# A scan and mixture-of-experts kernel: 64x64 quarters, 1/q0 by ScalarE, three routed groups

## The chip, the cores and the metric

The kernel runs on one core of a Trainium2 chip. A core has TensorE (PE: matmuls, with the weight load shown apart as PEld), VectorE (DVE), ScalarE (ACT), GpSimd (POOL) and SyncE (SP, which here only issues DMAs). Each engine works through its own instructions in the order in which they are written; between engines there are semaphores. Matmuls write to PSUM, which has eight banks of 512 fp32 values per partition; VectorE and ScalarE read it. The metric is device time in microseconds: three runs of the kernel before gave 320.64, 321.75 and 328.07 us, median 321.75.

## The reference, cut to what matters

```python
B, H, S, D = 4, 8, 768, 48                    # r, k, v, w: [B, H, S, D]; u: [H, D]
state = zeros(B, H, D, D)
for t in range(S):
    cur = einsum('bhd,bhe->bhde', u * k_t, v_t)
    y[:, :, t] = einsum('bhd,bhde->bhe', r_t, state + cur)
    state = w_t[..., None] * state + einsum('bhd,bhe->bhde', k_t, v_t)
x = y as rows: [B * S = 3072, H * D = 384]
skip = x @ w_skip > 0                         # only these rows are computed further
e = argmax(x @ w_gate); gate = softmax(x @ w_gate)[e]     # 8 experts
out = x + skip * gate * (relu(x @ w1[e]) @ w2[e])         # w1: 384 x 1024, w2: 1024 x 384
```

All tensors are fp32.

## The kernel before, in words

The recurrence is done in chunks of 128 positions: 4 batches of 6 chunks, 24 in all, all 8 heads at once. Within a chunk, `q` is the product of the decays w from a position to the chunk's end (a scan backwards, L277), `rh` the product from the chunk's start (a scan forwards, L289), `rq` = 1/q0 with q0 the whole chunk's product (L284). Then `kq` = k * q (L287, GpSimd), `rp` = r * rq * rh (L297, VectorE, one operation for each of the four head pairs), and the scores of a chunk are kq^T rp, masked to the positions before (L334). Tiles hold head pair a (0 to 3) in the free dimension and the two heads g of a pair in partitions 0 to 63 and 64 to 127, 48 rows of each in use.

A chunk's y comes together in one PSUM bank `psy`: VectorE first writes the bonus term there (L347: the sums over d of u r k, made by TensorE in bank `psb` from the block-diagonal ones-times-u tile `ubk_sb`, L343, times v transposed, `vt`), TensorE adds scores times v (L378, two heads side by side in the column halves of the array) and state times rp (L383, block-diagonal state `sblk`, the full array). ScalarE copies it out (`evict`, L388), TensorE turns it into rows and multiplies by the gate weights at once (`rows_out`, L396, two partial logits added later), and ScalarE and SP store the rows (`store`). The state lives in PSUM bank `psu` (L356 adds to it, L366 scales it by the next chunk's q0, L371 copies it into `sblk`).

The eight PSUM banks in this stage are psu, psY, psA0, psA1 (scores of heads g = 0 and 1), psB, pss (routing) and two of tag psT (transposes and rows).

The order on all engines is written out by hand (`manual_schedule`, L592 to L660): step s holds the state update and outputs of chunk s, the scores, masks and bonus of chunk s + 1, the scans of chunk s + 2, the loads of chunk s + 4, and the store of chunk s - 1. In step s VectorE's order is: scan q, reciprocal, scan rh, rp (for s + 2), two masks and the bonus (for s + 1). ScalarE's is: store copies (s - 1), state scalings and copies (s), the y copy (s), the transposed keys (s + 1), the check of w (s + 2). TensorE's is: state update, y (s), key transposes, scores and bonus sums (s + 1), rows (s). `later` holds routers, small chains of VectorE operations over a group of chunks that `drip(k)` emits between the others, k at a time; `flush` emits what they want of the other engines. `GROUPS` says after which chunks a router starts: after 6, 12, 18 and 24. For the first two groups the one-hot tiles of token positions are made by ScalarE (`mark`, two activations each, two chunks a step), for the others by VectorE (`one_hot`, L476). `beside` makes a GpSimd operation wait for a VectorE operation, so that the two don't begin at a bad time for each other: `rk` = r * k (L302) for the last rp, the weight split of L273 for the last routing operation.

After the 24 chunks the last group is routed beside the first expert's matmuls, and then the experts follow (L739 on): gathers of rows, matmuls in three passes of split weights, scatters. Their weights are loaded and split partly during the chunks (L652 to L660). That part uses the banks again, by their tags (L753).

## Time and profile before

| what | us |
|---|---|
| runs, median (lowest to highest) | 321.75 (320.64 to 328.07) |
| the profiled execution, whole | 317.5 |
| its span, first to last instruction | 315.6 |
| busy: TensorE, VectorE, ScalarE, GpSimd | 292.2, 244.8, 185.3, 115.5 |

The profile is of one execution. Lines such as L297 are lines of the kernel before. A busy time is the sum over instructions, of which successive ones can overlap; the mean of one is its whole duration. The chain of waits is followed back from the last instruction: at each step to what released it, or to the instruction before it on its engine; its rows are start, length, engine, tile written, line and number of instructions. In the rows of groups, the part after the second bar is the engine's idle time just before these instructions, and what ended it. fp32 matmuls are issued as two instructions each, so four matmuls show as x8. The granted clock of TensorE was 0.986 on average.

### The profile page before, as it was taken

The page shows a single profiled execution, that of the slowest core. Times are in us where ns is not written, and L with a number is a line of the kernel's source. Part 1 is how long each engine was busy: PE and PEld are TensorE (multiplying, and loading weights), DVE is VectorE, ACT ScalarE, POOL GpSimd, SP SyncE. Part 2 cuts the span into 40 slices and gives each one's busy share as a digit, 9 for nine tenths or more (in the row PEclk, how much of TensorE's full clock was granted, in tenths as well). Part 3 has the DMA queues.
Part 4 walks back from the last instruction along what each step waited for, and adds up shares of the span by engine and source line. Part 5 has one row for each costly group of instructions (what it writes and reads, how often), then busy time and mean ns, then how long its engine had stood idle before and what let it go on. Part 6 is the DMA issues. An engine that isn't in the chain of part 4 may idle for free.

```text
span 315.6 us, 8456 instructions
## 1 busy us (share of the span) xinstructions
PE 292.2 (93%) x3229; PEld 269.6 (85%) x3229; DVE 244.8 (78%) x505; ACT 185.3 (59%) x527; POOL 115.5 (37%) x118
## 2 busy tenths in 40 slices
PE   7499999899898998979999999999999999999992
PEld 2388888788787887868889899999999999999991
DVE  8899999999999999999637479587785949496310
ACT  4437667689775998766633358274564828184200
POOL 8164455555535566543401772411102020101111
PEclk9879999999999999999999999999999999999998
DMA  7999999999899988885301489756657473630001
GB/s 227 220 214 241 232 292 271 257 264 264 212 233 257 267 187 179 180 206 194 116 25 34 143 294 348 275 195 218 213 199 239 152 256 95 243 143 27 6 4 37
DMA packets 23778, 60.45 MB, mean 192 GB/s; under 512 B 4902, under 2 KB 11338, under 8 KB 23728
## 3 DMA queue, kind: packets, MB, share of 16 engines
q1 hardware_dynamic: 21248, 53.69, 62.6%
q0 software_dynamic: 2048, 5.48, 5.3%
q8 instruction: 27, 0.44, 0.7%
q10 hardware_dynamic: 432, 0.66, 0.6%
q14 instruction: 23, 0.19, 0.2%
HBM read 52.76 MB, written 7.86 MB: 192 GB/s over the span
## 4 chain that ended last, share of the span: by engine, by line
PE 72%; DMA 13%; DVE 10%; POOL 1%; issue 1%; ACT 1%; SPq 0%; POOLq 0%; DVEq 0%
DMA wrk<-wrk 10%; PE psO L790 7%; PE psO L788 7%; PE psO L789 7%; PE psY L378 6%; PE psH L770 6%; PE psH L769 6%; PE psH L768 6%; PE psA L328 6%; PE psY L383 5%; PE psB L343 5%; DVE asb L334 4%; PE psH L126 4%; DVE psY L347 3%; PE psT L321 3%; DVE rp L297 2%
## 5 line engine op out<-in xcount | busy, mean ns | idle before, releaser
L775 ACT ACTIVATE hh<-psH 128x256 fp32r<-128x256 f32 x60 | 23.0, 383 | 56.8 <-PE psH L770 53.5
L732 POOL DMA_INDIRECT out<-fin,ids x16 | 17.0, 1065 | 102.5 <-DVE fin L795 94.7
L770 PE MATMUL psH<-xTh,w1l 128*128 128x256 f32 x168 | 47.6, 283 | 0.0
L769 PE MATMUL psH<-xTl,w1h 128*128 128x256 f32 x168 | 47.6, 283 | 0.0
L768 PE MATMUL psH<-xTh,w1h 128*128 128x256 f32 x168 | 47.6, 283 | 0.0
L302 POOL TENSOR_TENSOR rk<-wrk 128x512 f32<-128x512 f32 x24 | 30.6, 1275 | 28.9 <-DVE rp L297 14.5
L788 PE MATMUL psO<-w2h,hh 128*128 128x384 f32 x120 | 40.8, 340 | 0.0
L790 PE MATMUL psO<-w2h,hl 128*128 128x384 f32 x120 | 40.2, 335 | 0.0
L789 PE MATMUL psO<-w2l,hh 128*128 128x384 f32 x120 | 40.2, 335 | 0.0
L378 PE MATMUL psY<-asb,v 128*48 128x128 f32 x384 | 26.6, 282 | 13.1 <-DVE psY L347 13.0
L287 POOL TENSOR_TENSOR kq<-wrk,q 128x512 f32<-128x512 f32 x24 | 28.6, 1190 | 18.5 <-DVE q L277 13.4
L776 DVE SCALAR_TENSOR_TENSOR hl<-psH,hh 128x256 fp32r<-128x256 f32 x60 | 25.2, 420 | 12.5 <-ACT hh L775 12.1
L334 DVE TENSOR_TENSOR asb<-psA,c_sb 128x512 f32<-128x512 f32 x48 | 30.7, 681 | 4.3 <-PE psA L328 4.3
L378 PEld LDWEIGHTS psY<-asb,v 128*48 128x48 f32 x384 | 20.5, 126 | 15.6 <-DVE psY L347 15.4
L297 DVE SCALAR_TENSOR_TENSOR rp<-wrk,rq,rh 128x128 f32<-128x128 f32 x96 | 33.1, 405 | 0.5
L770 PEld LDWEIGHTS psH<-xTh,w1l 128*128 128x128 f32 x168 | 32.2, 192 | 0.0
L769 PEld LDWEIGHTS psH<-xTl,w1h 128*128 128x128 f32 x168 | 32.2, 192 | 0.0
L768 PEld LDWEIGHTS psH<-xTh,w1h 128*128 128x128 f32 x168 | 32.2, 192 | 0.0
L795 DVE SCALAR_TENSOR_TENSOR fin<-psO,gates,xg 128x384 f32<-128x384 f32 x15 | 9.3, 618 | 28.5 <-PE psO L790 28.5
L289 DVE TENSOR_TENSOR_SCAN rh<-wrk,pss 128x516 f32<-128x516 f32 x24 | 28.9, 1205 | 2.6 <-PE pss L516 1.3
L277 DVE TENSOR_TENSOR_SCAN q<-wrk,pss 128x516 f32<-128x516 f32 x24 | 29.1, 1214 | 1.4 <-DMA wrk<-wrk 1.4
L343 PE MATMUL psB<-rk,ubk_sb 128*128 128x128 f32 x192 | 27.8, 288 | 0.9 <-POOL rk L302 0.9
(145 smaller groups left out, 668.6 us busy)
## 6 DMA issues: line engine op xcount, KB each, us to landing
r<-w SPq DMA_DIRECT2D x48, 512.0 KB, 5.8
wrk<-wrk SPq DMA_DIRECT2D x46, 288.9 KB, 6.3
v<-vN SPq DMA_DIRECT2D x24, 192.0 KB, 6.2
out<-x SPq DMA_DIRECT2D x24, 192.0 KB, 5.4
vt<-wrk SPq DMA_DIRECT2D x46, 96.0 KB, 6.1
wrk<-wrk SPq DMA_DIRECT2D x1, 258.5 KB, 3.8
wrk<-wrk ACTq DMA_DIRECT2D x1, 256.0 KB, 4.0
wrk<-wrk SPq DMA_DIRECT2D x1, 256.0 KB, 4.5
```

The lines of the kernel that those rows point to most:

```text
L277: nc.vector.tensor_tensor_scan(q.rearrange("p a j -> p (a j)")[:, ::-1], t[:, 1:1 + NP * CW][:, ::-1], floor, 0.0, op0=ALU.mult, op1=ALU.max)
L297: last = nc.vector.scalar_tensor_tensor(rp[:, a], wk["r"][:, a], wk["rq"][:, a], wk["rh"][:, a, :P], op0=ALU.mult, op1=ALU.mult)
L302: mul = nc.gpsimd.tensor_tensor(rk.rearrange("p a j -> p (a j)"), wk["w"][:, R_OFF:K_OFF], wk["w"][:, K_OFF:V_OFF], op=ALU.mult)
L334: nc.vector.tensor_tensor(s, psa[g], tri.rearrange("p (o j) -> p o j", o=1).to_broadcast([P, NP, P]), op=ALU.mult)
L343: nc.tensor.matmul(wk["psb"][:, a], ubk_sb[:, a], wk["rk"][:, a], start=True, stop=True)
L378: nc.tensor.matmul(psy[64 * g:64 * g + D, a], v[:, 2 * a + g], wk["asb"][g][:, a], start=False, stop=(c == 0), skip_group_check=True)
L768: nc.tensor.matmul(ps, w1h[:, o:o + P], xTh[:, kc], start=(kc == 0), stop=False)
L769: nc.tensor.matmul(ps, w1h[:, o:o + P], xTl[:, kc], start=False, stop=False)
L770: nc.tensor.matmul(ps, w1l[:, o:o + P], xTh[:, kc], start=False, stop=(kc == KC - 1))
L788: nc.tensor.matmul(pso, h[j, fc][0], w2h[:, o], start=(fc == 0), stop=False)
L789: nc.tensor.matmul(pso, h[j, fc][0], w2l[:, o], start=False, stop=False)
L790: nc.tensor.matmul(pso, h[j, fc][1], w2h[:, o], start=False, stop=(fc == FC - 1))
```

## The change

- **Quarters.** `ubk_sb` and `sblk` lose their zero blocks (64 columns, not 128). The bonus sums (L343) and state times rp (L383) become eight matmuls each on 64x64 quarters of the array, where they were four on the full array.
- **y in two banks.** `psy` becomes a bank for each g (tags psY0, psY1), with head pair a = 2 * c2 + a2 at partition half c2 and column block a2. To pair with this, `vt` is laid out so too (four loads per chunk where there were two, each in pieces of 1 KB where there were 2 KB, issued one step later), `wgp_sb` as well (twelve loads at the start where there were three), and `store` puts the columns back. The bonus and the y copy become two operations each, one for each bank. The score matmuls of L378 are ordered by bank.
- **The bonus sums' place.** The bank psB goes: the sums are written into columns 64 to 127 of each head pair in psA0 and psA1, after the masks have read these. `bonus_sums` and `bonus` move from step s - 1 to step s, after the state update, and the bonus stands ahead of the scan q on VectorE.
- **1/q0 by ScalarE.** `scale_reads` makes r * rq by four ScalarE activations, after `evict` in ScalarE's order; VectorE then makes rp by one tensor_tensor with rh in place.
- **Order.** `rows_out` moves from the end of step s to the start of step s + 1. `intra` is split: `turn` (key transposes and their copy) comes ahead of the outputs, `scores` where `intra` was.
- **State copy.** One ScalarE copy of 128x192 in place of two of 64x192.
- **Routers.** Groups of 9, 9 and 6 chunks. All one-hots by VectorE; `mark` goes. `drip`'s pace at the late group is 3, before 2. The split of L273 waits for the bonus of its step, in place of the last routing operation.

```diff
-GROUPS = ((0, 6), (6, 6), (12, 6), (18, 6))
+GROUPS = ((0, 9), (9, 9), (18, 6))
+GM = 9
...
+        def load_vt(i):
+            b, c = seq[i]
+            vt = vt_sb[i % (NBUF + 1)]
+            for c2 in range(2):
+                for g in range(2):
+                    o = V_OFF + 2 * c2 * P
+                    nc.sync.dma_start(vt[64 * c2:64 * c2 + D, 2 * g:2 * g + 2],
+                                      wrk[b, c, g, :, o:o + 2 * P])
...
-        psy = ps1.tile([P, NP, P], F32, tag="psY", name="psY")
+        psy = [ps1.tile([P, 512], F32, tag=f"psY{g}", name=f"psY{g}") for g in range(2)]
+        psy3 = [z[:, :2 * P].rearrange("p (b j) -> p b j", b=2) for z in psy]
...
-                mul = nc.gpsimd.tensor_tensor(lo, raw, hi, op=ALU.subtract)
-                if vec.last is not None:
-                    beside(mul, vec.last)
+                beside(nc.gpsimd.tensor_tensor(lo, raw, hi, op=ALU.subtract), work[i - 2]["bonus"])
...
-        def prep_reads(i):
+        def scale_reads(i):
             wk = work[i]
             rp = wk["rp"] = att.tile([P, NP, P], F32, tag="rp", name=f"rp{i}", bufs=3)
             for a in range(NP):
-                last = nc.vector.scalar_tensor_tensor(
-                    rp[:, a], wk["r"][:, a], wk["rq"][:, a], wk["rh"][:, a, :P],
-                    op0=ALU.mult, op1=ALU.mult)
+                nc.scalar.activation(rp[:, a], wk["r"][:, a], AF.Copy, scale=wk["rq"][:, a])
+
+        def prep_reads(i):
+            wk = work[i]
+            rp = wk["rp"]
+            last = nc.vector.tensor_tensor(rp, rp, wk["rh"][:, :, :P], op=ALU.mult)
...
+        psb = [z.rearrange("p a (h j) -> p a h j", h=2)[:, :, 1] for z in psa]
+
         def bonus_sums(i):
-            wk = work[i]
-            wk["psb"] = ps1.tile([P, NP, P], F32, tag="psB", name=f"psB{i}")
-            for a in range(NP):
-                nc.tensor.matmul(wk["psb"][:, a], ubk_sb[:, a], wk["rk"][:, a],
-                                 start=True, stop=True)
+            rk = work[i]["rk"].rearrange("p a (h j) -> p a h j", h=2)
+            for a2 in range(2):
+                for c2 in range(2):
+                    for g in range(2):
+                        a, rows = 2 * c2 + a2, slice(64 * g, 64 * g + HP)
+                        nc.tensor.matmul(psb[g][64 * c2:64 * c2 + HP, 2 * a2:2 * a2 + 2],
+                                         ubk_sb[rows, a], rk[rows, a], start=True, stop=True)
 
         def bonus(i):
-            nc.vector.tensor_tensor(psy, work[i]["psb"], vt_sb[i % (NBUF + 1)], op=ALU.mult)
+            vt = vt_sb[i % (NBUF + 1)].rearrange("p a (h j) -> p (a h) j", h=2)
+            for g in range(2):
+                work[i]["bonus"] = nc.vector.tensor_tensor(
+                    psy[g][:, :2 * P].rearrange("p (q j) -> p q j", j=HP), psb[g],
+                    vt[:, 4 * g:4 * g + 4], op=ALU.mult)
...
             if c > 0:
-                for a in range(NP):
-                    nc.tensor.matmul(psy[:, a], sblk[i % 2][:, a], wk["rp"][:, a],
-                                     start=False, stop=True, skip_group_check=True)
+                for a2 in range(2):
+                    for c2 in range(2):
+                        for g in range(2):
+                            a, rows = 2 * c2 + a2, slice(64 * g, 64 * g + HP)
+                            nc.tensor.matmul(psy3[g][64 * c2:64 * c2 + D, a2],
+                                             sblk[i % 2][rows, a, :D], wk["rp"][rows, a],
+                                             start=False, stop=True, skip_group_check=True)
 
         def evict(i):
-            xT = work[i]["xT"] = att.tile([P, NP, P], F32, tag="xT", name=f"xT{i}")
-            nc.scalar.copy(xT, psy)
+            xT = work[i]["xT"] = att.tile([P, 2 * 2, P], F32, tag="xT", name=f"xT{i}")
+            for g in range(2):
+                nc.scalar.copy(xT[:, 2 * g:2 * g + 2], psy3[g])
...
                 if on(s - 1):
+                    rows_out(s - 1)
                     store(s - 1)
+                if on(s):
+                    update(s)
+                    carry(s)
+                    bonus_sums(s)
+                drip(pace[0])
                 for i0, m in GROUPS:
                     if i0 + m == s:
-                        pace[0] = 1 if i0 + m < LATE else 2
+                        pace[0] = 1 if i0 + m < LATE else 3
                         later.append(router(i0, m))
                         if i0 + m == LATE:
                             later.append(early())
                 if on(s):
-                    update(s)
-                    carry(s)
-                drip(pace[0])
+                    bonus(s)
                 if on(s + 2):
                     prep_scan(s + 2)
+                if on(s + 1):
+                    turn(s + 1)
+                flush()
                 if on(s):
                     outputs(s)
-                flush()
                 if on(s + 2):
                     prep_keys(s + 2)
                     drip(2 * pace[0])
-                    prep_reads(s + 2)
                 if on(s):
                     evict(s)
+                if on(s + 2):
+                    scale_reads(s + 2)
+                    prep_reads(s + 2)
                 if on(s + 1):
-                    intra(s + 1)
+                    scores(s + 1)
                     mask(s + 1, 0)
                     mask(s + 1, 1)
-                    bonus_sums(s + 1)
-                    bonus(s + 1)
                     drip(2 * pace[0])
                 if on(s + 2):
                     prep_check(s + 2)
-                for _ in range(min(2, len(marks))):
-                    marks.popleft()()
                 if s == n - 1:
                     early_tokens(0)
-                if on(s):
-                    rows_out(s)
                 flush()
```

162 lines of the change are left out of this document (75 added, 87 removed).

## The prediction

> **What bounds the kernel now.** I read the engine totals first, then a table of stretches, then the chain of waits, then the groups by shape and a timeline of two steps.
>
> ```profile
> span 315.6 us, 8456 instructions
> PE 292.2 (93%) x3229; PEld 269.6 (85%) x3229; DVE 244.8 (78%) x505; ACT 185.3 (59%) x527; POOL 115.5 (37%) x118
> ...
> 15.00:60.00 45.00, 43.00 (x642) 37.91 (x643) 42.73 (x83) 28.99 (x96) 24.18 (x21) 0.94 1.05 253
> 60.00:100.00 40.00, 36.89 (x580) 31.96 (x579) 38.37 (x79) 31.97 (x101) 21.05 (x20) 1.00 1.00 249
> 100.00:140.00 40.00, 36.15 (x552) 31.65 (x553) 38.68 (x83) 31.78 (x105) 21.62 (x20) 1.00 0.90 198
> ```
>
> The last three rows are stretches of the scan stage (columns: length, busy time of PE, PE weight load, DVE, ACT, POOL, then granted clock, DMA share, GB/s). TensorE and VectorE are both nearly full there, ScalarE is busy for 64% to 80%, and the DMA share is near one. So nothing has much room, and shortening one engine helps only until the next thing is late. The chain shows one undisturbed step and where the stage begins and ends:
>
> ```profile
> 16.05 1.95 PE psY L378 x16
> ...
> 22.98 0.88 PE psY L378 x16
> 23.86 1.09 PE psY L383 x8
> ...
> 25.38 1.02 PE psA L328 x24
> 26.40 1.09 PE psB L343 x8
> ...
> 28.86 0.88 PE psY L378 x16
> ...
> 56.89 0.62 DVE psY L347
> 57.55 1.08 PE psY L378 x16
> ...
> 63.95 6.65 DMA wrk<-wrk
> 70.62 7.75 DMA wrk<-wrk
> ...
> 160.96 1.08 PE psY L378 x16
> ```
>
> From 22.98 to 28.86 the chain is TensorE alone (the three pieces left out are its transposes, rows and state updates): an early step is 5.88 us of matmuls without a hole. The first y matmul of chunk 0 is at 16.05 and that of chunk 23 at 160.96: 23 steps in 144.9 us, 6.30 us each. The first seven, up to 57.55, took 41.5 us (5.93 each); the other sixteen, with routers in the drips, took 103.4 us (6.46 each), and there VectorE and DMA pieces interleave in the chain. The stage after 163 us is expert work, which the change leaves alone but for the names of two banks. Everything is decided in these 23 steps.
>
> **The change part by part.** *Quarters.* L383 (y from the state) and L343 (the bonus sums) each cost 1.09 us in the chain: 8 instructions on the full array. Each becomes 16 instructions on 64x64 quarters, cycling through the four quarters. The row for quarters is L328: 32 instructions in 1.02 us, 0.032 each, so 16 cost 0.51. Of L328's instructions half are 64 columns long; if columns set the pace, 16 of full length cost 0.68. If four side by side halve the pace of L378's pairs (16 in 0.88), they cost 0.44. I take 0.51, the form nearest by shape. TensorE thus loses 0.58 us for the sums and, on the 20 chunks with a state, 0.58 for y: a step of 5.88 becomes 4.72, and TensorE stops being the bound.
>
> ```profile
> PEld psY L383 <- issue: 3.7, 20, 0.2
> ```
>
> In this table of waits (us in total, times, longest) the weight load of L383 idles 0.2 us each time the array goes from 128x48 to 128x128 stationary tiles. The Trainium skill, "TensorEngine Tiling (Array Packing)", Key Properties, says that changing the tiling mode drains TensorE, which agrees with this row and speaks against a schedule that mixes quarters, halves and full tiles. By that rule each of the two changed groups would cost one such 0.2 more, 0.4 us a step, and the forecast below would be some 9 us higher. The sum goes by the row, with 0.2 once, in the fresh start below.
>
> *1/q0 onto r by ScalarE.* VectorE's four multiplies at L297 become one tensor_tensor over 128x512, and ScalarE gets four activations of 128x128 with a per-partition scale.
>
> ```profile
> L334 DVE TENSOR_TENSOR asb<-psA,c_sb 128x512 f32<-128x512 f32 x48 | 30.7, 681 | 4.3 <-PE psA L328 4.3
> L776 DVE SCALAR_TENSOR_TENSOR hl<-psH,hh 128x256 fp32r<-128x256 f32 x60 | 25.2, 420 | 12.5 <-ACT hh L775 12.1
> L205 DVE TENSOR_SCALAR hot<-iota,rall 128x256 bf16<-128x256 bf16 x12 | 2.6, 283 | 0.1
> L775 ACT ACTIVATE hh<-psH 128x256 fp32r<-128x256 f32 x60 | 23.0, 383 | 56.8 <-PE psH L770 53.5
> L366 ACT ACTIVATE psu<-psu,q 128x48 f32<-128x48 f32 x80 | 22.2, 278 | 2.5 <-PE psu L356 0.3
> L311 ACT ACTIVATE junk<-wrk,bias_lo 128x512 bf16<-128x512 f32 x24 | 17.5, 730 | 1.5 <-DMA wrk<-wrk 1.5
> L408 ACT COPY x<-psX 128x192 f32<-128x192 f32 x48 | 13.1, 329 | 0.0
> L482 ACT ACTIVATE dd<-iota,rall 128x256 bf16<-128x256 bf16 x12 | 6.0, 503 | 0.0
> ...
> 28.27 1.22 DVE L277 TENSOR_TENSOR_SCAN q<-wrk,pss 128x516 f32<-128x516 f32 x1
> 28.47 0.55 ACT L408 COPY x<-psX 128x192 f32<-128x192 f32 x2
> 28.97 1.20 ACT L366 ACTIVATE psu<-psu,q 128x48 f32<-128x48 f32 x4
> 29.52 0.18 DVE L284 RECIPROCAL rq<-q 128x4 f32<-128x4 f32 x1
> 29.62 1.20 DVE L289 TENSOR_TENSOR_SCAN rh<-wrk,pss 128x516 f32<-128x516 f32 x1
> 30.85 1.14 DVE L297 SCALAR_TENSOR_TENSOR rp<-wrk,rq,rh 128x128 f32<-128x128 f32 x4
> 31.19 1.09 PE L328 MATMUL psA<-rp,kq 64*64 64x128 f32 x32
> 32.35 1.29 DVE L334 TENSOR_TENSOR asb<-psA,c_sb 128x512 f32<-128x512 f32 x2 [0.35 <-PE psA L328]
> ```
>
> On VectorE the four multiplies take 1.14 us. One 128x512 operation takes 0.61 when another follows (two masks 1.29, less one of 0.681), so 0.53 is saved; the bonus as two halves of about 0.42 (the 128x256 row), overlapping, costs 0.75 for 0.69. VectorE's own step is then 0.75 + 1.22 + 0.1 (rq, overlapped) + 1.20 + 0.61 + 1.29, about 5.2 us, and some 5 router operations when a router runs.
>
> One scaling on ScalarE: the two rows with a per-partition operand give 503 ns for 256 columns and 730 for 512, hence 390 for 128. Successive operations overlap: two x copies of 329 ns take 0.55, so 0.11 is shared. Four are 4 x 0.39 - 3 x 0.11 = 1.23 us; without overlap, as the four psu scalings show (1.20 for 4 x 278 ns), 1.56. I take 1.23, as separate output tiles are like the x copies; 0.9 (four plain copies at the rate of x, shortened) is the low end. The Trainium skill, "ScalarE: Activation LUTs", What ACT_TABLE_LOAD costs, gives 186 ns + 0.833 ns per column + 93 ns for a pointer operand, with 93 ns of overlap; an estimate from it is 1.27 us for four, and the 503 ns row agrees (492); by it the forecast would move by 1 us. The same page's Rules for kernel authors send multiplies to VectorE, not ScalarE.
>
> ScalarE's total stays bearable: 28.99 us in 45 is 3.8 per step; plus 1.23, plus 0.07 for y's eviction in two halves, less about 0.3 for one state copy in place of two, is 4.8, and under 6 with a weight cast and a routing op.
>
> *The new order, where the gain is lost.* The step's order now has these waits in a ring: VectorE's masks of chunk s+1 read both psA banks; the bonus sums of s+1 are written into columns 64 to 127 of those same banks, so TensorE waits for the masks; VectorE's bonus waits for the sums; the y matmuls wait for the bonus; ScalarE's eviction waits for y; **the scaling for s+2/s+3 stands behind the eviction on ScalarE**; rp on VectorE waits for the scaling; and the next masks stand behind rp on VectorE. Before, the sums had a bank of their own and rp needed only VectorE. The ring, once round:
>
> - masks to TensorE 0.04 (57.51 to 57.55 in the chain); the sums 0.51, plus 0.20 because a start after a wait costs that (L378 is 1.08 there, 0.88 without); to VectorE 0.07 (L328 ends at 32.28, L334 starts at 32.35): 0.82
> - first half of the bonus 0.42, to TensorE 0.04: 0.46
> - y: L378 0.98 (between 0.88 and 1.08, as transposes run just ahead), L383 0.51, to ScalarE 0.03: 1.52
> - eviction and scaling: 2 x 0.383 + 4 x 0.39 - 5 x 0.11 = 1.78, to VectorE 0.04: 1.82
> - rp and two masks: 0.61 + 1.29 = 1.90
>
> Sum 6.52 us. Against it VectorE reaches rp after 0.75 + 1.22 + 0.1 + 1.20 = 3.3 us from the bonus's start, and the scaling only after 0.46 + 1.52 + 1.82 = 3.8: VectorE idles 0.5 there and 0.8 between masks and bonus. So the 0.58 + 0.58 + 0.53 us taken off are spent waiting. Behind the waiting rp stand the masks and all routing drips; behind the waiting sums stand the transposes and y.
>
> Ends for the ring: low 5.9 (quarters at 0.44, no fresh start, scaling 0.9), high about 7.3 (quarters at 0.68, scaling 1.56, L378 at 1.08 and a drain or two of 0.2).
>
> *Routers.* The three groups save one pass of about 16 small operations (some 0.2 us each, between rq's 0.18 and the one-hot's 0.28, so 3.2) and put twelve one-hots more on VectorE: 12 x 0.283 = 3.4. Level; and at pace 1 they fall into VectorE's two holes. ScalarE loses the 24 marking operations (12 us), which it did beside other work. At pace 3, for about three steps from chunk 18, up to fifteen small operations lie in a step: nine between masks and next bonus (about 1.9 us against a hole of 0.8) and six before rp (1.2 against 0.5): 1 to 2 us a step, less what pace 2 cost before; I count +3 in all (0 to 5).
>
> *Loads.* v transposed comes in four DMAs per chunk, not two, with pieces of 1 KB instead of 2, and one step later; it is needed two steps after that.
>
> ```profile
> 29.47 1.31 SPq L155 DMA_DIRECT2D vt<-wrk  x2
> r<-w SPq DMA_DIRECT2D x48, 512.0 KB, 5.8
> wrk<-wrk SPq DMA_DIRECT2D x46, 288.9 KB, 6.3
> v<-vN SPq DMA_DIRECT2D x24, 192.0 KB, 6.2
> out<-x SPq DMA_DIRECT2D x24, 192.0 KB, 5.4
> vt<-wrk SPq DMA_DIRECT2D x46, 96.0 KB, 6.1
> ```
>
> Two more issues add up to this row's 1.3 us to SP's step; behind them on SP stand v, the store and the weight piece, each wanted a step or more later. Nine more small loads of wgp at the start lie ahead of chunk 3's load, which is not wanted until step 1. A step moves 2 x 288.9 + 192 + 192 + 2 x 96 = 1,154 KB, with a weight piece 1,666 KB, 1.71 MB: at 6.52 us that is 262 GB/s, just above the 249 to 253 of the stretches, so the twelve steps with weights may each wait about 0.2 us: +2. The setup's lost memset and copy are beside the first loads: nothing.
>
> *Ends of the stage.* The first y starts later by the sums that now stand in the path (0.8, less 0.3 saved on rp: +0.5); the last y is 0.58 shorter.
>
> **The sum.** 23 x 6.52 = 150.0; four of these steps have a chunk without a state, 4 x 0.51 = 2.0 less: 148.0. Plus 3 (pace), 2 (loads), 0.5 - 0.5: 153 against 144.9, +8. The profiled execution took 317.5 us (span 315.6 and 1.9 around), so its counterpart is 325.5. The runs' median, 321.75, is 4.25 above that execution; on the runs' scale the forecast is 329.5, 2.4% slower.
>
> **The rivals.** *Faster: the ring is short, and the engines' own sums bind.* If the links sit at their low ends, the ring is 5.9; if besides y's first bank is evicted while the second is still being written (one half of the eviction, 0.27), it is about 5.65, and VectorE's 5.2 plus router work is level with it: 23 x 5.65 = 130, less 2, plus 3 and, as the loads are then pressed harder, 4: 135 against 144.9, 10 less: 312. For it: TensorE and VectorE are the two full engines and both get work taken off. Against: each link is in the written order. It decides from a ring under 5.8. Chance 0.21.
>
> *No change: a ring of 5.8 to 6.4*, by shorter overheads on ScalarE, no fresh start and quarters at 0.44: 315 to 327. The masks with rp, y and the eviction alone are 1.9 + 1.3 + 0.65, which no reading shortens, so this takes 0.1 to 0.7 off the other 2.7. Chance 0.28.
>
> *Slower still: quarters don't run four side by side*, as when two row halves meet in one bank or the modes' drains add up: 0.2 to 0.4 more per group, two groups, 20 steps and more: +8 to +16 on the forecast, 338 to 345. The psA row, with the same pattern of quarters and banks, is against it. *Or loads*: the weight steps of 63.95 to 78.37, where two wrk transfers of 6.65 and 7.75 stand in the chain, get worse with twice the pieces: +1 us on twelve steps, 340. Together 0.09.
>
> The forecast itself, a ring of 6.4 to 6.9 (327 to 338), has 0.42; its lowest part, 0.06, is still within 2%. About 2% (315.3 to 328.2) is what a measurement here tells from no change. So: faster 0.21, within 2% 0.28 + 0.06 = 0.34, slower 0.36 + 0.09 = 0.45. The range 313 to 340 leaves out about one tenth on each side; the forecast's own is 327 to 338.
>
> **What would show it.** In the new profile TensorE's busy share between 15 and 160 us falls below 0.85 and its groups L383 and L343 halve; VectorE shows idle time before rp released by ScalarE (about 0.5 us in most steps) and before the bonus released by TensorE (0.6 to 0.8); ScalarE's scalings start where the eviction ends; the distance between y matmuls is 6.4 to 6.7, early steps as long as late ones. It is wrong if rp waits for nothing, if the early steps are under 6.0 us, or if DMA releases most of the waits.

## The result, and the profile after

Four runs of the changed kernel took 350.01 to 355.18 us, median 352.62; four of the kernel before 320.64 to 328.38 us, median 324.91. The ratio is 1.098, with a 95% interval of 1.084 to 1.112: the change makes the kernel slower, and by four times the 2.4% that were forecast. The profiled execution took 352.67 us (span 350.9), where that of the kernel before had taken 317.5 (315.6).

The totals, and the same three stretches as before (columns as there):

```profile
span 350.9 us, 9257 instructions
PE 299.1 (85%) x3579; PEld 263.3 (75%) x3579; DVE 233.6 (67%) x455; ACT 196.0 (56%) x597; POOL 113.6 (32%) x114
...
15.00:60.00 45.00, 36.67 (x580) 28.85 (x582) 30.01 (x48) 26.14 (x92) 17.38 (x15) 0.81 0.85 188
60.00:100.00 40.00, 33.34 (x594) 26.44 (x584) 31.68 (x57) 30.99 (x108) 20.19 (x17) 0.96 0.99 237
100.00:140.00 40.00, 32.95 (x630) 26.25 (x628) 32.77 (x63) 31.38 (x111) 19.91 (x20) 1.00 0.90 213
```

No engine is full any more: between 100 and 140 us TensorE is busy for 82% where it was 90%, VectorE for 82% where it was 97%. In the first stretch the granted clock fell from 0.94 to 0.81. One undisturbed step, from y of chunk 17 to y of chunk 18, in the timeline of the changed kernel (start, busy time, engine, line, operation; the bracket is the idle time before, and who ended it):

```profile
139.36 1.08 PE L393 MATMUL psY<-asb,v 128*48 128x128 f32 x16
...
140.37 0.65 PE L401 MATMUL psY<-rp,sblk 64*48 64x128 f32 x16
...
141.08 0.65 ACT L408 COPY xT<-psY 128x256 f32<-128x256 f32 x2 [1.04 <-PE psY L401]
141.61 1.28 ACT L297 ACTIVATE rp<-wrk,rq 128x128 f32<-128x128 f32 x4
...
142.92 0.69 DVE L302 TENSOR_TENSOR rp<-rp,rh 128x512 f32<-128x512 f32 x1 [0.83 <-ACT rp L297]
...
143.53 1.28 DVE L340 TENSOR_TENSOR asb<-psA,c_sb 128x512 f32<-128x512 f32 x2
...
144.36 1.17 PE L354 MATMUL psA<-rk,ubk_sb 64*64 64x128 f32 x16 [0.91 <-DVE asb L340]
...
145.46 0.65 PE L324 MATMUL psT<-c_sb,kq 128*128 128x128 f32 x4
145.57 0.77 DVE L360 TENSOR_TENSOR psY<-psA,vt 128x256 f32<-128x256 f32 x2 [0.76 <-PE psA L354]
...
146.06 0.32 PE L393 MATMUL psY<-asb,v 128*48 128x128 f32 x2
```

Read downwards, each row waits for the one above: y, eviction, scaling, product, masks, sums, bonus, y again, 6.70 us after the first (139.36 to 146.06). This is the ring that the prediction wrote down, each link at its place.

The place of y's first matmul in each chunk divides every trace into a start, 23 steps and a tail:

| profiled execution | whole | first y | 23 steps | tail after the last y |
|---|---|---|---|---|
| before, first shown | 317.5 | 16.05 | 144.9 | 154.7 |
| after | 352.67 | 19.15 | 165.7 | 166.1 |
| before, once more (experiment below) | 327.95 | 16.57 | 145.3 | 164.2 |

So 3.1 us of the 35.3 came from the start, 20.8 from the steps, and 11.4 from the tail. The third row shows that the last of these is not the change's: the kernel before has the longer tail too, in an execution of 327.95 us, and the first profile happened to be one without it. The steps of the changed kernel in order, in us: 6.97 9.00 8.02 6.70 7.33 7.58 6.10 6.70 6.70 6.72 7.46 7.48 6.15 6.69 7.24 6.70 6.70 6.70 8.95 9.65 8.30 6.70 5.18. The undisturbed step is 6.70 (5.88 before), 6.10 to 6.15 in steps 7 and 13, where a batch begins and y from the state is left out, and 5.18 for the last; what lies above it is mostly in steps 2 to 6 and 19 to 21, and less in 11, 12 and 15.

### The profile page after: what moved, and what is told of

Its sections match the earlier page's. It is cut to its first block, busy times and chain, and to the rows that moved or that the text cites. A ratio compares the mean times of both kernels' runs of the same rounds, so it can differ in the third digit from the quotient of the medians.

```text
span 350.9 us, 9257 instructions
## 1 busy us (share of the span) xinstructions
PE 299.1 (85%) x3579; PEld 263.3 (75%) x3579; DVE 233.6 (67%) x455; ACT 196.0 (56%) x597; POOL 113.6 (32%) x114
## 4 chain that ended last, share of the span: by engine, by line
PE 47%; DMA 28%; DVE 7%; ACT 5%; SPq 5%; issue 2%; another core or an unknown queue 2%; POOL 2%; ACTq 0%; POOLq 0%; DVEq 0%
DMA wrk<-wrk 21%; PE psH L785 6%; PE psH L784 6%; PE psH L786 6%; PE psO L804 6%; PE psO L806 6%; PE psO L805 6%; DMA vt<-wrk 4%; PE psH L127 3%; ACT rp L297 2%; DVE asb L340 2%; PE psY L393 2%; SPq L158 2%; SPq L618 2%
## 5 line engine op out<-in xcount | busy, mean ns | idle before, releaser
L791 ACT ACTIVATE hh<-psH 128x256 fp32r<-128x256 f32 x60 | 23.0, 383 | 68.2 <-PE psH L786 52.6
L354 PE MATMUL psA<-rk,ubk_sb 64*64 64x128 f32 x384 | 26.8, 307 | 24.2 <-DVE asb L340 22.1
L804 PE MATMUL psO<-w2h,hh 128*128 128x384 f32 x120 | 42.1, 351 | 2.5 <-ACT hh L791 2.3
L805 PE MATMUL psO<-w2l,hh 128*128 128x384 f32 x120 | 41.4, 345 | 1.1 <-issue 1.1
L806 PE MATMUL psO<-w2h,hl 128*128 128x384 f32 x120 | 41.6, 347 | 0.0
L792 DVE SCALAR_TENSOR_TENSOR hl<-psH,hh 128x256 fp32r<-128x256 f32 x60 | 25.2, 420 | 24.5 <-ACT hh L791 20.8
L354 PEld LDWEIGHTS psA<-rk,ubk_sb 64*64 64x64 f32 x384 | 15.5, 143 | 31.9 <-issue 24.3
L287 POOL TENSOR_TENSOR kq<-wrk,q 128x512 f32<-128x512 f32 x24 | 28.3, 1178 | 26.5 <-DVE q L277 26.1
L784 PEld LDWEIGHTS psH<-xTh,w1h 128*128 128x128 f32 x168 | 33.0, 196 | 0.0
L297 ACT ACTIVATE rp<-wrk,rq 128x128 f32<-128x128 f32 x96 | 30.7, 398 | 3.9 <-DVE rq L284 3.6
L393 PE MATMUL psY<-asb,v 128*48 128x128 f32 x384 | 30.0, 306 | 3.1 <-DVE psY L360 3.1
L408 ACT COPY xT<-psY 128x256 f32<-128x256 f32 x48 | 15.9, 376 | 29.7 <-PE psY L401 28.5
L302 DVE TENSOR_TENSOR rp<-rp,rh 128x512 f32<-128x512 f32 x24 | 16.6, 691 | 22.8 <-ACT rp L297 22.7
```

Source lines behind the costliest of these rows:

```text
L297: nc.scalar.activation(rp[:, a], wk["r"][:, a], AF.Copy, scale=wk["rq"][:, a])
L354: nc.tensor.matmul(psb[g][64 * c2:64 * c2 + HP, 2 * a2:2 * a2 + 2], ubk_sb[rows, a], rk[rows, a], start=True, stop=True)
L393: nc.tensor.matmul(psy3[g][64 * c2:64 * c2 + D, a2], v[:, 2 * a + g], wk["asb"][g][:, a], start=False, stop=(c == 0), skip_group_check=True)
L784: nc.tensor.matmul(ps, w1h[:, o:o + P], xTh[:, kc], start=(kc == 0), stop=False)
L804: nc.tensor.matmul(pso, h[j, fc][0], w2h[:, o], start=(fc == 0), stop=False)
L805: nc.tensor.matmul(pso, h[j, fc][0], w2l[:, o], start=False, stop=False)
```

## The experiments

All in one table first. The clean step is the length that most undisturbed steps share; start, steps and tail are from the profiled execution, the whole is the median where there were several runs.

| label | whole | first y | 23 steps | clean step | tail |
|---|---|---|---|---|---|
| scale_first | 344.39 | 18.86 | 160.0 | 6.16 | 163.7 |
| sums_by_g | 349.63 | 18.84 | 163.8 | 6.68 | 165.2 |
| ring_cut | 346.50 | 20.86 | 158.9 | 6.48 | 164.9 |
| q0_vector | 346.85 | 19.83 | 159.9 | 6.41 | 165.3 |
| scores_ahead | 351.29 | 23.15 | 162.7 | 6.15 | 163.7 |
| sa2 (4 runs) | 332.23 | 19.62 | 158.5 | 6.00 | 154.0 |
| sa3 (4 runs) | 325.40 | 19.41 | 150.5 | 5.1-5.5 | 155.1 |
| few_loads | 350.38 | 18.89 | 164.1 | 6.70 | 165.4 |
| start_sync | 358.90 | 19.49 | 171.3 | 6.70 | 166.4 |
| pace2 | 354.77 | 18.88 | 168.5 | 6.70 | 165.6 |
| groups6 | 349.16 | 19.66 | 161.2 | 6.70 | 166.5 |
| drip_behind | 355.00 | 19.61 | 178.9 | 6.70 | 154.7 |
| shift80 | 351.98 | 20.64 | 165.0 | 6.70 | 164.6 |
| gather_late | 345.12 | 20.46 | 167.5 | 6.70 | 155.4 |
| after_gl3 (4 runs) | 342.21 | 19.74 | 164.9 | 6.70 | 155.3 |
| before_gl (10 runs) | 317.36 | 16.25 | 144.6 | 5.88 | 153.9 |
| before_gl2 (4 runs) | 317.72 | 16.47 | 144.9 | 5.88 | 154.9 |

The clean step repeats to 0.02 us. The 23 steps together do not: five executions with the same loop (after, shift80, gather_late, after_gl3, start_sync) lie between 164.9 and 171.3, and single steps of 9 to 12 us come and go with loads that land late. Only the clean step and the named steps are compared below.

### Is it a ring?

**scale_first** puts ScalarE's scaling ahead of its eviction.

```diff
-                if on(s):
-                    evict(s)
                 if on(s + 2):
                     scale_reads(s + 2)
+                if on(s):
+                    evict(s)
+                if on(s + 2):
                     prep_reads(s + 2)
```

> The changed kernel with one swap: ScalarE's four scalings for chunk s+2 stand ahead of the y eviction of chunk s. Ring theory: the eviction (0.65 us) leaves the ring; what is left goes over VectorE, bonus 0.75, scan q 1.22, rq 0.1, scaling 1.23, rp and two masks 1.9, the wait for the sums 0.8 and some 0.1 of semaphores, 6.1 us, so undisturbed steps go from 6.70 to 6.1 and the run from 352 to about 341. Rival, that the steps are paced by loads or by TensorE's granted clock: they stay at 6.7 and the run within 3 us.

The clean step fell to 6.16 us. One exchange of two neighbours on an engine that is busy 56% of the time took 0.54 us off every clean step, as the ring has it. Loads and TensorE's granted clock, the rival, would have left it at 6.7.

**sums_by_g** orders the bonus sums by bank, so that the first half of the bonus can start after eight of them.

```diff
-            for a2 in range(2):
-                for c2 in range(2):
-                    for g in range(2):
+            for g in range(2):
+                for a2 in range(2):
+                    for c2 in range(2):
```

> The changed kernel with the bonus sums ordered by bank: all eight instructions of head group 0 first, then those of group 1, so that the first half needs only the first mask. Ring theory: the first half runs beside the second mask, VectorE's hole between masks and bonus falls from 0.8 to 0.3 us, undisturbed steps from 6.70 to 6.2, the run to about 342. Rival: with two quarters in use instead of four the sums take twice as long (0.9 us for 0.55), and the hole stays; steps at 6.7.

A miss: 6.68 us. VectorE's wait ahead of the bonus fell from 0.76 to 0.24 us, as meant, but y started 1.23 us after the masks where it had been 1.25. In the rows above one sees why: behind the sums on TensorE stand the transposes of the next chunk (145.46 to 146.1), ahead of y. The ring has two strands there, VectorE's bonus and TensorE's transposes, and both are 1.25 us long.

**ring_cut** does both and moves the transposes ahead of the state update.

```diff
+                if on(s + 1):
+                    turn(s + 1)
                 if on(s):
                     update(s)
...
-                if on(s + 1):
-                    turn(s + 1)
                 flush()
```

> Scaling ahead of the eviction, the bonus sums ordered by bank, and the four transposes of the next chunk moved ahead of the state update, so that between the masks and the y matmuls TensorE has only the sums. Theory 'ring': from the end of the masks to y it takes the 8 sums of one bank and one bonus product (about 0.25 + 0.39 us) where it was 1.25, so the undisturbed step falls from 6.16 to 5.5-5.6 us and the whole to about 330 us. Rival 'the transposes and sums were not in the ring, TensorE's own work or VectorE's sets the step': 6.1 to 6.2 us stays, about 344 us.

A miss again, 6.48: worse than scale_first alone. One step of it, in the timeline:

```profile
67.53 0.65 PE L401 MATMUL psY<-rp,sblk 64*48 64x128 f32 x16
...
68.17 1.28 ACT L297 ACTIVATE rp<-wrk,rq 128x128 f32<-128x128 f32 x4 [0.56 <-DVE rq L284]
...
69.36 0.62 ACT L408 COPY xT<-psY 128x256 f32<-128x256 f32 x2
...
69.76 1.14 PE L416 MATMUL psX<-wgp_sb,xT 128*128 128x105 f32 x8 [0.72 <-ACT xT L408]
...
70.74 0.60 PE L324 MATMUL psT<-c_sb,kq 128*128 128x128 f32 x4
...
71.27 0.56 PE L371 MATMUL psu<-v,kt 128*48 128x48 f32 x16
...
71.77 0.68 PE L354 MATMUL psA<-rk,ubk_sb 64*64 64x128 f32 x16
...
72.52 0.76 DVE L360 TENSOR_TENSOR psY<-psA,vt 128x256 f32<-128x256 f32 x2 [1.08 <-ACT psu L381]
```

The masks of this step end at 71.44 (70.17 + 1.27), yet the sums start only when rows, transposes and state update are done. The eviction, in its turn, waits no longer for y, which is done at 68.18 (67.53 + 0.65), but for the scaling that now stands ahead of it. The moved transposes joined another ring: eviction, rows, transposes, update, sums, bonus, then VectorE's scan and reciprocal, the scaling, and the eviction again. Taking a link out of one ring had put it into the next.

**q0_vector** undoes one part: 1/q0 goes onto r by VectorE as before; all else is as changed.

```diff
-                nc.scalar.activation(rp[:, a], wk["r"][:, a], AF.Copy, scale=wk["rq"][:, a])
+                last = nc.vector.scalar_tensor_tensor(
+                    rp[:, a], wk["r"][:, a], wk["rq"][:, a], wk["rh"][:, a, :P],
+                    op0=ALU.mult, op1=ALU.mult)
...
-            last = nc.vector.tensor_tensor(rp, rp, wk["rh"][:, :, :P], op=ALU.mult)
```

> The changed kernel with 1/q0 put onto r by VectorE as in the kernel before (four operations of about 0.39 us, no scaling on ScalarE), quarters, two banks and groups as changed. Theory 'ring': the hop eviction, scaling, product goes, but VectorE now has 0.77 + 1.22 + 0.18 + 1.20 + 1.54 + 1.28 = 6.2 us of work per step and still waits 0.76 us for the sums, which stand behind the masks: step 6.9 to 7.0 us, whole about 357. Rival 'the scaling on ScalarE is what made the change slow': step 5.9 to 6.3 us, whole about 335-343.

The step was 6.41, between the two. The expectation counted four multiplies at 4 x 0.39; overlapped they take 1.14, as the first profile had shown, and with that its sum is 6.5. So the scaling on ScalarE costs 0.29 us a step (6.70 against 6.41). What remains from 5.88 to 6.41 is probably the sums' new place, as VectorE, now nearly alone in the ring, still waits 0.81 us between masks and bonus; no run moved the sums alone.

**scores_ahead** changes only the order: scores of chunk s + 1 ahead of y of chunk s, its masks behind the first scan, the sums first on TensorE. **sa2** evicts ahead of the scaling, keeps the old order for chunk 0, and has few_loads and gather_late (below). **sa3** puts the reciprocal and the scaling ahead of the masks and of the eviction. The excerpt shows the new order, without the conditions for chunk 0 and the lines that it replaces.

```diff
                 if on(s):
+                    bonus_sums(s)
+                if on(s - 1):
+                    rows_out(s - 1)
+                    store(s - 1)
+                if on(s + 1):
+                    turn(s + 1)
+                if on(s):
+                    update(s)
+                    carry(s)
...
                 if on(s + 1):
+                    scores(s + 1)
                 if on(s):
                     outputs(s)
                 flush()
+                if on(s + 2):
+                    prep_recip(s + 2)        # sa3
+                    scale_reads(s + 2)       # sa3
+                mask(s + 1, 0)
+                mask(s + 1, 1)
                 if on(s):
                     evict(s)
```

> The changed kernel with another order on the engines alone: the scores of chunk s+1 ahead of the y matmuls of chunk s, its masks right behind the first scan, the bonus sums first on TensorE and rows, transposes and state update behind them, the scaling ahead of the eviction. Theory 'the step of 6.70 us is a ring through y, eviction, scaling, product, masks, sums and bonus, and no engine's work': with the ring cut to masks, sums, bonus and scores (1.28 + 0.7 + 0.77 + 1.1 us and about 0.4 of handing over) the undisturbed step falls to what TensorE and VectorE have to do, 5.4 to 5.8 us, and the whole to 326-332 us. Rival 'quarters are dearer work in themselves': 6.2 us or more. Tail and start as they were.

> Scores ahead of y from chunk 1 on as in scores_ahead, but the eviction ahead of keys and scaling (there it stood 1.1 us behind its matmuls, for the scaling, and the ring had become y, scaling, eviction, rows, transposes, update, scores: 6.15 us); chunk 0 in the old order; with few_loads and gather_late. Theory 'ring': the clean step falls by that 1.1 us until TensorE's work sets it, 5.4 to 5.8 us; first y 18.5 to 20.5, tail 155, late steps some 5 us over: 308 to 318 us, faster than the kernel before. Rival 'the quarters and the ScalarE scaling cost in themselves': step 6.1 us or more, 322 us or more.

> As sa2, with the reciprocal right behind the first scan, the scaling right behind it and ahead of the eviction, so that ScalarE scales while VectorE masks and the product waits for nothing. In sa2 the ring was y, eviction, scaling, product, bonus, scores (6.00 us, VectorE idle 0.95 us ahead of the product). Theory 'ring': that 0.95 goes but for 0.3 us of hand-overs, 5.3-5.6 us where nothing else is late; loads and routing keep their extras (some 15 us over the 23 steps), whole 318 to 326. Rival 'quarters cost 6 us of TensorE and ScalarE work whatever the order': 5.9 to 6.1 us, whole 329 to 335.

They gave 6.15, 6.00 and 5.1 to 5.5 us: the first two miss the 5.4 to 5.8 that were expected. In scores_ahead the eviction stood behind a scaling that itself waited for masks and reciprocal: scaling, eviction, rows, transposes, update, scores and masks were the ring. In sa2 it was eviction, scaling, product, bonus and scores, with VectorE idle 0.95 us ahead of the product. In sa3 no ring is left in undisturbed steps. The stretch from 25 to 45 us of it, without routing and weights (columns as above):

```profile
25.00:45.00 20.00, 19.81 (x412) 16.54 (x411) 18.24 (x31) 17.63 (x65) 8.56 (x7) 1.00 0.93 197
```

TensorE is busy 19.81 us of 20. The quarters with all their side conditions are thus 5.2 us of TensorE's work where the kernel before had 5.88; the order in which the change put them made 6.70 of it. As a whole sa2 is slower than the kernel before it ran beside (332.23 against 317.70; ratio 1.044, 1.038 to 1.049). Whether sa3 (319.62 to 326.95 us) is faster than the kernel before it ran beside (328.88) is unclear: by its two shorter runs the ratio is 0.980 (0.971 to 0.988), which lies across 2%. And it has the gathers moved, and the kernel before with that one edit is faster still (317.72). Its steps 19 to 21 took 11.44, 10.24 and 8.89 us, and steps 14 and 15 took 9.39 and 7.21, so that most of what the clean steps gained was lost there.

### Early loads and the start

**few_loads** brings v transposed in two DMAs per chunk and the gate weights in one, laid out by the host.

```diff
-                for g in range(2):
-                    nc.sync.dma_start(vt[64 * c2:64 * c2 + D, 2 * g:2 * g + 2],
-                                      wrk[b, c, g, :, o:o + 2 * P])
+                nc.sync.dma_start(vt[64 * c2:64 * c2 + D].rearrange("p (g e) j -> p g (e j)", g=2),
+                                  wrk[b, c, :, :, o:o + 2 * P].rearrange("g d x -> d g x"))
...
-                    for q in range(4):
...
+                    nc.sync.dma_start(wgp_sb, wgp)
```

> The changed kernel with fewer DMAs for the same bytes: v transposed in two DMAs per chunk (pieces still of 1 KB), the gate weights in one DMA from an array that the host lays out, in place of twelve. Load theory (the count of DMAs on SP's queue, each of which waits for an earlier one, delays the start): first y at about 16.5 us in place of 19.15, the second to seventh steps (9.00, 8.02, 6.70, 7.33, 7.58 us) at about 6.7 each, TensorE's half-clock windows in the first 60 us gone but for the first; the run 7 to 9 us shorter, about 344. Rival, that the 1 KB pieces themselves are slow: only the start gets shorter, by 3 us. Neither theory expects a change in the stretch from the last y to the end (166.1 us, before the change 154.7).

The first six steps were 6.71 6.69 6.70 6.70 7.34 6.70, 40.8 us where they had been 45.6. What had stood there is in the changed kernel's chain (SPq is SyncE issuing DMAs; L616 and L618 are the twelve gate loads, L158 a chunk's load):

```profile
6.79 7.95 DMA wrk<-wrk
...
14.76 0.56 SPq L618
...
22.71 0.51 SPq L158
...
23.26 4.91 DMA wrk<-wrk
```

SyncE issues a gate load about every 0.6 us from 14.76 on (one takes 1.91), and chunk 3's load comes behind them at 22.71. The run changes the v loads as well; that it is the gate loads is read from this chain. The start did not move (18.89), against the expectation, and the whole gained only 2.3 us, as steps 19 and 20 of that execution took 9.73 and 10.30.

**start_sync** lets SyncE issue chunk 0's four v loads, in place of ScalarE.

```diff
-                        nc.scalar.dma_start(vt[64 * c2:64 * c2 + HP, 2 * g:2 * g + 2],
+                        nc.sync.dma_start(vt[64 * c2:64 * c2 + HP, 2 * g:2 * g + 2],
```

> The changed kernel with chunk 0's four v loads issued by SyncE in place of ScalarE. Theory 'the four issues ahead of ScalarE's first operations make the start late': the first y comes at 17.0 to 17.8 us where it came at 18.9 to 19.2. Rival 'the start waits for chunk 1's keys on GpSimd, or for TensorE at half clock': 18.8 to 19.3 us. Whole 350 to 353 us by both.

A miss. ScalarE's first scaling came at 6.67 us, 1.5 earlier, but the first y at 19.49. Two other things were as late as before:

```profile
12.14 1.23 DVE L277 TENSOR_TENSOR_SCAN q<-wrk,pss 128x516 f32<-128x516 f32 x1 [3.33 <-DMA wrk<-wrk]
...
16.85 0.40 POOL L666 CAST iota<-c_sb 128x256 bf16<-128x256 f32 x1 [6.60 <-DMA c_sb<-cst]
...
17.21 1.18 POOL L287 TENSOR_TENSOR kq<-wrk,q 128x512 f32<-128x512 f32 x1
...
18.44 1.11 PE L324 MATMUL psT<-c_sb,kq 128*128 128x128 f32 x4 [0.45 <-POOL kq L287]
```

Chunk 1's keys (L287) stand on GpSimd behind a cast that waits for constants until 16.85, and y of chunk 0 now stands behind the transposes of these keys. In the kernel before the cast came as late (16.11), but only chunk 1 waited for it. This is read from the rows; no run moved the cast.

### The late steps

**pace2** drips two routing operations at a place, as the kernel before, in place of three; **groups6** goes back to four groups of six; **drip_behind** puts the operations that stood between second scan and product behind the masks.

```diff
-                        pace[0] = 1 if i0 + m < LATE else 3      # pace2: else 2
-GROUPS = ((0, 9), (9, 9), (18, 6))                               # groups6: four of six
...
                     prep_keys(s + 2)
-                    drip(2 * pace[0])                            # drip_behind
...
                     mask(s + 1, 1)
-                    drip(2 * pace[0])
+                    drip(4 * pace[0])                            # drip_behind
```

> The changed kernel with the late router's pace at 2, as before the change. Ring theory: VectorE's holes hide about five small operations a step; at pace 3 up to fifteen lie in a step, at pace 2 ten. The three long steps after chunk 18 (8.95, 9.65, 8.30 us) fall to about 7.7 each and one or two more steps get longer by 0.5; the run 2 to 4 us shorter. Rival: the same operations only spread over more steps, no difference within 1 us.

> The changed kernel with four routed groups of six chunks in place of 9, 9 and 6, one-hot rows still on VectorE. Theory 'the second group of nine, drained at pace 3 in the last five steps, makes steps 19 to 21 long (8.95, 9.65 and 8.30 us)': with six chunks fewer operations and matmuls are drained there, the three steps sum to 22-23 us where they were 26.9, and the whole is about 348. Rival 'any routing in these steps holds the ring up as much, since each wait of TensorE for a routing operation of VectorE is the same': 26 to 27 us, whole 352. The tail stays 164 to 166 us by both.

> The changed kernel with the routing operations that stood on VectorE between the second scan and the product of the reads put behind the masks instead. In step 20 of the changed kernel seven of them (148.71 to 150.40 us, 1.7 us) stand there, ahead of product and masks. Theory 'the late steps are long because routing stands in the ring': steps 19 to 21, 26.9 us together in the changed kernel's profile and 28.5 in two later ones, fall to 22-24 us, whole 347-350 (with the tail's stall). Rival 'the operations cost the same wherever they stand': 26.5 to 28.5 us.

Steps 19 to 21 summed to 26.9 us in the changed kernel, and to 29.1 with pace2 (with step 22 at 9.2 besides), 25.1 with groups6 and 30.5 with drip_behind. The five executions with the changed loop gave 26.9 to 28.5, so pace2 lies hardly outside of them. Fewer operations helped by 1.8 us or more, less than foretold; the other place made it worse by 2 us or more, so the theory that they hurt only by standing ahead of the product fell. The rows of step 19 (y of chunk 18 to y of chunk 19; the expectation calls it 20), of VectorE and of TensorE, in the changed kernel:

```profile
148.71 0.29 DVE L439 TENSOR_TENSOR lg<-lgs 128x81 f32<-128x81 f32 x1
...
150.25 0.23 DVE L459 TENSOR_TENSOR oh<-key,km 128x72 bf16<-128x72 f32 x1
150.40 0.68 DVE L302 TENSOR_TENSOR rp<-rp,rh 128x512 f32<-128x512 f32 x1
...
150.53 0.19 PE L462 MATMUL pss<-oh,trib 128*128 128x72 bf16 x1 [2.38 <-DVE oh L459]
...
150.81 1.61 PE L416 MATMUL psX<-wgp_sb,xT 128*128 128x105 f32 x8
...
151.00 1.28 DVE L340 TENSOR_TENSOR asb<-psA,c_sb 128x512 f32<-128x512 f32 x2
...
152.34 0.88 PE L371 MATMUL psu<-v,kt 128*48 128x48 f32 x16
153.16 1.13 PE L354 MATMUL psA<-rk,ubk_sb 64*64 64x128 f32 x16
...
154.34 0.76 DVE L360 TENSOR_TENSOR psY<-psA,vt 128x256 f32<-128x256 f32 x2 [1.46 <-PE psA L354]
```

and of drip_behind:

```profile
160.59 0.19 PE L462 MATMUL pss<-oh,trib 128*128 128x72 bf16 x1 [4.62 <-DVE oh L459]
...
164.61 0.77 DVE L360 TENSOR_TENSOR psY<-psA,vt 128x256 f32<-128x256 f32 x2 [3.48 <-PE psA L354]
```

Seven operations of the router, up to the one that makes `oh`, stand ahead of the product on VectorE (1.7 us). The matmul that reads `oh` (L462) stands on TensorE ahead of rows, state update and sums, so TensorE waits for `oh` and the sums come behind it. Move the operations behind the masks, and TensorE waits 4.62 us in place of 2.38: both ends of the router are in the ring. Step 19 is 2.25 us over the clean 6.70, and the rows divide it: 0.78 us come ahead of the product (4.34 us from y's start at 146.06, where the clean step has 3.56), 1.30 between masks and bonus (152.28 to 154.34, where it has 0.76), and 0.17 behind that. (Chunk 18 begins a batch; against the 6.10 of such a step the first part is 1.4.) In the second part the matmuls are slow besides: rows, update and sums took 1.61, 0.88 and 1.13 us here, 1.14, 0.56 and 0.68 in the step of ring_cut above, as TensorE's granted clock was 0.5 from 151.3 on (last section).

Step 19 holds ten routing operations on VectorE, but not each of them costs its length. The three behind the masks (152.20 to 152.88) are over long before the bonus starts. At pace 1 steps 10 to 14 of after_gl3 hold 22 such operations, three to six each, and take 6.72, 6.70, 6.70, 6.15 and 6.70 us: there the holes hide them. They cost where many stand ahead of the product, or where TensorE waits for one of them. In the kernel before, step 19 holds seven such operations and takes 6.79 us, between neighbours with three (6.82) and six (6.45): VectorE had slack there.

### The tail

At the head of the experts ScalarE evicts four hidden-layer groups (L791; L775 before). In the first profile they come at 178.03, 179.32, 180.66 and 182.00. In the changed kernel, TensorE's and ScalarE's rows are these:

```profile
199.88 5.62 PE L127 MATMUL psH<-xT,r 128*128 128x128 f32 x48
...
202.96 0.38 ACT L791 ACTIVATE hh<-psH 128x256 fp32r<-128x256 f32 x1 [3.36 <-PE psH L127]
...
207.94 0.38 ACT L791 ACTIVATE hh<-psH 128x256 fp32r<-128x256 f32 x1 [4.09 <-PE psX L743]
...
212.88 0.38 ACT L791 ACTIVATE hh<-psH 128x256 fp32r<-128x256 f32 x1 [4.06 <-remote]
...
217.18 0.38 ACT L791 ACTIVATE hh<-psH 128x256 fp32r<-128x256 f32 x1 [3.41 <-remote]
```

The 48 matmuls are recorded in 5.6 us, as before, but what waits for them is let go 4.3 to 5 us apart. TensorE's semaphore, which these evictions wait for, counts up at 202.88, 207.91, 212.86 and 217.16, and then twice more within 0.1 us for two groups of transposes written behind: the counts come late, in a row. In the twelve profiled executions with such a stall the last of the four came 2.5 to 3.9 us after the last of GpSimd's gathers in a row was issued.

**before_again** is the kernel before, unchanged. **shift80** has 80 small matmuls ahead of chunk 0's state update, which move TensorE's instruction blocks.

> The kernel before, unchanged, profiled once more: its times shown so far lie near 321 and near 328 us, and the profiled execution was 317.5. Theory 'the tail's stall belongs to the change': last y to end 154.7 us again, the four hidden-layer evictions at the head of the experts 1.3 us apart, half clock 11 us in all. Rival 'the stall also comes to the kernel before, in its slower executions': in an execution of 325 us or more these evictions stand 4 to 6 us apart, the tail is 160 to 166 us, and there is a half-clock window of 7 to 14 us in it.

> The changed kernel with 80 small matmuls (16 columns) ahead of chunk 0's state update, where TensorE waits 3.5 us for the masks. They move each 16 KB block of TensorE's instructions 160 instructions ahead, so that the block which now is fetched at 199.9 us, among the gathers (195 to 215 us), is fetched ahead of them, as in the kernel before (169.2, gathers from 171.2). Theory 'the tail's stall hangs on that fetch': last y to end falls from 166.1 to about 155 us, the whole to about 341. Rival 'the stall has nothing to do with it': tail 164 to 166, whole 351 to 354 (the start 0 to 1 us later).

The rival was right in the first: an execution of 327.95 us has the stall, without any change.

```profile
178.97 0.38 ACT L775 ACTIVATE hh<-psH 128x256 fp32r<-128x256 f32 x1 [2.29 <-PE psH L126]
...
184.67 0.38 ACT L775 ACTIVATE hh<-psH 128x256 fp32r<-128x256 f32 x1 [4.81 <-PE psX L727]
...
191.09 0.38 ACT L775 ACTIVATE hh<-psH 128x256 fp32r<-128x256 f32 x1 [5.52 <-remote]
...
194.72 0.38 ACT L775 ACTIVATE hh<-psH 128x256 fp32r<-128x256 f32 x1 [2.74 <-remote]
```

In the second, TensorE's block of instructions now came at 189.7, ahead of the gathers (195.8 on), and the stall stayed (evictions 7.1, 5.7 and 2.9 us apart, tail 164.6): it does not hang on that fetch.

**gather_late** and **after_gl3** (the changed kernel), **before_gl** and **before_gl2** (the kernel before) issue four gathers at the experts' head and the other ten two at a time, one expert or more ahead of their use.

```diff
-        for s in range(2, 2 * E):
+        for s in range(2, 6):
             gather(s, moe)
...
         def expert(e):
+            for s in (2 * e + 6, 2 * e + 7):
+                if s < 2 * E:
+                    gather(s, moe)
```

> The changed kernel with only four of its fourteen later token gathers at the head of the experts; the other ten are issued two at a time at the start of each expert, one expert and more ahead of their use. Theory 'TensorE's signals are held up as long as GpSimd's row of gathers runs' (in every execution with the stall it ended 2.6 to 3.2 us after the last of these gathers): the stall is gone or under 3 us, tail 153 to 157 us, whole 340 to 344. Rival 'the gathers only run beside it': tail 163 to 167 us, whole 350 to 354.

> The kernel before with only the gathers moved, as in gather_late. Theory 'the stall at the head of the experts is a matter of the gathers and in the kernel before it comes in most executions, not all': tail 153 to 156 us, every execution within 2 us of 316 to 319, ratio to the kernel before 0.965 to 0.985. Rival 'the later gathers cost the experts what the stall cost': 322 to 328, ratio 0.99 to 1.01.

> The changed kernel with the gathers moved, timed against the kernel before. Theory 'start and the 23 steps alone make the change slow': tail 153 to 157 in every execution, 340 to 347 us; the ratio is 1.07 to 1.09 where the kernel before runs without its stall (316 to 319 us) and 1.04 to 1.06 where it has it (about 327). Rival 'the tail is part of the change': executions of 350 us and more come back.

> The kernel before with the gathers moved, once more, since in the session of its first comparison the kernel before never stalled. Theory 'the stall hangs on the row of gathers': 315 to 318 us in every execution, whether the kernel before beside it stands at 317 or at 327. Rival 'the stall comes with the session or the chip, whatever the order of the gathers': where the kernel before stands at 327, this one does too.

With the edit the tail was 153.9 to 155.4 in all four profiles. before_gl could show nothing of the stall, as in its session the kernel before, by its times, never had it (thirteen runs, 316.77 to 319.17; ratio 0.999, 0.998 to 1.001): the edit costs nothing. In that session drip_behind, the changed kernel with its row of gathers whole, had no stall either (tail 154.7): the row alone doesn't bring it, and the change doesn't. In the session of after_gl3 and before_gl2 the kernel before had it in each of seven runs, by their times (328.25 to 329.40), and before_gl2 beside it took 317.10 to 318.22: ratio 0.966, interval 0.964 to 0.968. That is the version that beats both kernels. after_gl3 beside the same runs was slower (ratio 1.039, 1.035 to 1.044). What is left of the stall ends again some 2 us after the last gather of the short row:

```profile
178.53 0.38 ACT L778 ACTIVATE hh<-psH 128x256 fp32r<-128x256 f32 x1 [2.20 <-PE psH L126]
...
182.82 0.39 ACT L778 ACTIVATE hh<-psH 128x256 fp32r<-128x256 f32 x1 [3.40 <-PE psX L727]
...
183.61 0.39 ACT L778 ACTIVATE hh<-psH 128x256 fp32r<-128x256 f32 x1
...
184.39 0.40 ACT L778 ACTIVATE hh<-psH 128x256 fp32r<-128x256 f32 x1
```

(before_gl2; its sixth and last gather of the row was issued at 180.70.) The change by itself, the stall taken out on both sides, is therefore 341.71 us (the median of those three runs of after_gl3 that agree within 0.7%) against 317.72: 7.6% slower, 24.0 us.

## Why the prediction was wrong

It said 329.5 us (its terms add up to 329.75), 8 us over the runs' median, with a range to 340. Slower was right and the ring was right. What failed is the sum: four of its terms were too small, TensorE's clock was taken at nothing, and the stall in the tail was not in it at all. By the two stall-free profiles (339.9 and 316.3 us of span) the change costs 3.3 us in the start, 20.0 in the steps and 0.4 in the tail, where the sum had 0.5, 8.1 and -0.5. The 20.0 are 6.5 of the ring (151.4 against 144.9), 7.0 in the late steps, 3.2 in steps 2 and 3, 2.7 of half clock in steps 5, 6 and 17, and 0.55 in step 15.

- *The ring, 6.52 us: right.* Measured 6.70, link by link in the clean step: y 1.72 (forecast 1.52), eviction and scaling 1.84 (1.82), product and masks 1.89 (1.90), masks to bonus 0.76 (0.82), bonus to y 0.49 (0.46). Only y was off: the scores' part took 1.01 (139.36 to 140.37) for 0.98, and the state matmuls take 0.71 to the eviction's start (140.37 to 141.08), not 0.54. VectorE's two idle places were forecast at 0.5 and 0.8 and are 0.83 and 0.76. 23 steps by this ring, with 6.10 and 6.15 for steps 7 and 13 and 5.18 for the last, are 151.4 us, where the sum had 148.0: 3.4 of the miss. (The high end of the ring, "about 7.3", is what its terms give without a drain; with the one or two that it names it is 7.5 to 7.7.)
- *One strand of the ring was overlooked.* Masks to y was counted through the bonus alone; the transposes on TensorE are as long. It changed nothing in the sum, but sums_by_g failed for it.
- *"I count +3 in all (0 to 5)" for pace 3: measured +7.0* (steps 19 to 21 of the stall-free profile: 8.49, 10.10, 8.50). That VectorE's holes hide operations was right at pace 1. At pace 3 the wait that the routing puts on TensorE, ahead of rows, update and sums, was not in the count, nor the half clock in these steps.
- *Loads, "+2": measured +3.2* in steps 2 and 3 (8.61 and 8.02). The place was wrong: not the weight steps but the twelve gate loads, which were said to lie "ahead of chunk 3's load, which is not wanted until step 1". At about 0.6 us an issue they hold that load until 22.7 us, and it is late.
- *The start, +0.5: measured +3.3.* The sums in the path were counted; not that y of chunk 0 now stands behind chunk 1's transposes, whose keys wait on GpSimd.
- *TensorE's clock was no term at all.* The forecast's TensorE has waits in every step, and nothing asked what a wait does to the matmuls behind it. In steps 3, 6 and 17 of after_gl3's profile y takes 2.9 to 3.0 us from its first matmul to the eviction, where it is 1.72, each time at half clock, and nothing else in these steps is late: 3.8 us, of which 1.3 stand under the loads above. The 0.55 of step 15, another term that was missing, is a wait of TensorE (0.75 us) for a routing operation.
- *The stage after 163 us, "which the change leaves alone": right*, but the profile that the forecast was laid against was an execution without the stall, while the runs' median stood between both kinds. The 4.25 us between the two, which the forecast carried along as a constant, are probably a part of this stall (no execution near 321 us was profiled); the four executions of the changed kernel lie 8 to 13 us above after_gl3's 342.21 and so probably hold it too, as the profiled one does.

Of the forecast's signs, most came: TensorE's share fell below 0.85 (102.96 us of the 125 in the three stretches), VectorE idles ahead of product and bonus for the engines named, the scalings start where the eviction ends, and the distance of y is 6.70. Two did not: the early steps were longer than the later ones, and the two groups of matmuls did not halve. That of L383 fell from 23.2 to 14.0 us of busy time and that of L343 from 27.8 to 26.8, as its first two instructions now start a mask ahead of the others. Of the rivals, steps under 5.8 exist (sa3) but in another order than the change's. The quarters did run four side by side (0.48 us from one group's start to the next, 140.37 to 140.85, where the sum took 0.51). The weight load's idle 0.2 us came no more often than before: ahead of L401 and L324 (19 and 15 times in the stage), where it had been ahead of L383, L343 and L328 (19, 20 and 19).
